# A Hedgehog linear-attention and Mish MLP block: the head rebuilt around ScalarE's roots, loads re-queued and held, three later orders changed

## The chip, the core and the metric

One Trainium2 chip, one core. The metric is the device time of one execution in microseconds (us); lower is better. TensorE is called PE, VectorE DVE, ScalarE ACT, GpSimd POOL; SyncE (SP) only issues DMAs here, and ACT has a DMA queue of its own beside its compute.

## What is computed

For x of 2048 tokens by 512 channels (bf16), with 32 heads of 16:

```python
xn = layernorm(x)                                  # eps 1e-5
q, k, v = split(xn @ wqkv)                         # 32 heads of 16
pq, pk = q @ w_phi[h], k @ w_phi[h]                # per head, 16x16
phi = concat(softmax(p), softmax(-p))              # for q and for k, 32 features
kv, z = sum over tokens of phi_k^T v, phi_k        # no causal mask
o  = (phi_q @ kv) / (phi_q @ z + 1e-6)
h  = xn @ w1 + b1                                  # 512 -> 1792
out = x + o @ wo + mish(h) @ w2                    # mish(h) = h*tanh(softplus(h))
```

## The kernel before

**Tiles and groups.** The tokens are 16 tiles of 128 (`x_sb[:, t, :]`), in NG = 4 groups of TPG = 4. xn is needed transposed (`xnT`); the first group is transposed on PE (`ln_turn_pe`: four 128x128 transposes into a PSUM bank, then a copy), the others by DMA (`ln_turn_dma`).

**Folded weights.** w_phi acts per head, so `fold` multiplies the keys' part of wqkv (loaded transposed by DMA, `load_turned`, tile `wT`) with a block-diagonal w_phi (`Wbd`, the product of a 0/1 mask `block` and the loaded `wsrc`). The result `wkp` gives pk directly from xn: `logits(s, i)` is four accumulating matmuls (`project`) and a cast to `p_sb`. Later `wqp` is made alike for the queries. Steps s = 0 to 3 are the keys' groups, s = 4 to 7 the queries' groups.

**Softmaxes.** `extremes(s)` finds each head's maximum and minimum by a tree on DVE and writes p - max and min - p to `e`; `exponentials` runs Exp on ACT in halves of two tiles (and, for the queries, `turn` transposes each tile by DMA into `qT`); `normalise` sums and divides on DVE for the keys. `accumulate` sums kv in PSUM.

**MLP.** `hidden(n)` does the next n of 56 units: four matmuls with w1 and a Mish on ACT, per 128 hidden channels and group of tokens. They are the filler between the attention's steps: 5, then for s = 0 6+6+5, then 14, 8, 10, and 2 after the last group. `second_layer(t, f0, f1)` adds 128x512 matmuls with w2 for tile t.

**Second phase.** A half h is two tiles. `attend(h, i)` makes numerator and denominator in four PSUM banks (`pnd`, one buffer) and ACT copies them out; `combine` divides on DVE and transposes by DMA (`ob`); `project_out(h)` adds the product with wo, `residual` adds x on DVE, and `store` issues what waits.

**Order.** The order on each engine is the order of the program (a manual schedule): nothing is reordered. PSUM banks come from pools in fixed rotations: a matmul into a bank waits until the copy of its last use is done. In the second phase the second-layer blocks and the projections rotate over four banks (`ps`).

**The head** (lines 438 to 494). SP issues tiles 0 and 1 of x, then the transposed keys' weights, then tiles 4 to 7, wv, w1 and tiles 8 to 15. ACT issues w_phi, tiles 2 and 3, and b1. PE runs 12 warm-up matmuls on the identity (L466) until the data are there. Variance to 1/sqrt runs on POOL (L131: add eps, L134: power of -0.5); DVE makes `Wbd` (L472). Then PE does the fold (L110), transposes of tiles 0 and 1 (L152), the first projection (L168), the transposes of tiles 2 and 3, three more projections, the values (from 13.11 us) and the hidden units.

Of the kernel before, what the change touches and what calls it, by code (L numbers as in the profile page):

```python
# [9 lines left out]
BF16 = mybir.dt.bfloat16  # L10
# [8 lines left out]
def kernel(  # L19
# [13 lines left out]
    P = 128  # L33
# [54 lines left out]
    wo_sb = wqk[:, :, D : 2 * D]  # L88
    ident = consts.tile([P, P], BF16, name="ident")
    mhalf = consts.tile([P, TPG], FP32, name="mhalf")  # L90
    block = consts.tile([P, 8, 16], BF16, name="block")
    KVmask = consts.tile([P, 34], FP32, name="KVmask")
    vext = [vpool.tile([P, TPG, 4, 4, 36], BF16, name=f"vext{i}") for i in range(2)]
# [5 lines left out]
    def load_turned(base_col):  # L99

        wT = lnp.tile([P, 4, 512], BF16, name="wT", tag="xn")
        nc.sync.dma_start_transpose(out=wT[:], in_=A_wqkv[:, base_col : base_col + D])
        return wT

    def fold(wT, dst, dve):

        for kt in range(KT):
            pf = bank("pfold")
            for j in range(4):
                nc.tensor.matmul(  # L110
                    pf[:, j * P : (j + 1) * P],
                    lhsT=wT[:, j, kt * P : (kt + 1) * P],
                    rhs=Wbd[:, j, :],
                    start=True,
                    stop=True,
                )
            if kt in dve:
                nc.vector.tensor_copy(dst[:, kt, :], pf[:])
            else:
                nc.scalar.copy(dst[:, kt, :], pf[:])  # L120

    def ln_stats(t0, n):

        stats = lnp.tile([P, TPG, nc.vector.BN_STATS_DIM], FP32, name="stats")
        mv = lnp.tile([P, TPG, nc.vector.BN_AGGR_DIM], FP32, name="mv")
        rstd = lnp.tile([P, TPG], FP32, name="rstd")
        for i in range(n):
            nc.vector.bn_stats(stats[:, i, :], x_sb[:, t0 + i, :])  # L128
        for i in range(n):
            nc.vector.bn_aggr(mv[:, i, :], stats[:, i, :])  # L130
        nc.gpsimd.tensor_scalar(  # L131
            out=rstd[:, 0:n], in0=mv[:, 0:n, 1], scalar1=1e-5, scalar2=None, op0=ALU.add
        )
        nc.gpsimd.tensor_tensor(out=rstd[:, 0:n], in0=rstd[:, 0:n], in1=mhalf[:, 0:n], op=ALU.pow)  # L134
        return mv, rstd
# [24 lines left out]
            in_=xn[:, i : i + 2, :].rearrange("p t c -> p (t c)"),  # L160
        )

    def project(w, t, pp=None):

        if pp is None:
            pp = bank("pproj")[:]
        for kt in range(KT):
            nc.tensor.matmul(  # L168
                pp, lhsT=xnT[:, t, kt, :], rhs=w[:, kt, :],
                start=(kt == 0), stop=(kt == KT - 1),  # L170
            )
        return pp
# [65 lines left out]
                    op=ALU.subtract,  # L238
                )

    def exponentials(s, ks=(0, 1)):
        for k in ks:
            v = e_of[s][:, 2 * k : 2 * k + 2, :, :]
            nc.scalar.activation(v, v, ACT.Exp)  # L244
            if s >= NG:
                turn(s, k)

    def turn(s, k):

        qT = epool.tile([P, 2, 8, P], BF16, name="qT", bufs=3)  # L250
        qT_of[2 * (s - NG) + k] = qT
        for i in range(2):
            nc.sync.dma_start_transpose(
                out=qT[:, i, :, :],
                in_=e_of[s][:, 2 * k + i, :, :].rearrange("p l c -> p (l c)"),
            )

    def normalise(s, k, between=None):

# [155 lines left out]
    def project_out(h):  # L415
        for t in (2 * h, 2 * h + 1):
            for po, c in zip(po_of.pop(t), halves(t)):
                for j in range(4):
                    nc.tensor.matmul(  # L419
                        po[:, c], lhsT=oT_of[h][:, t % 2 * 4 + j, :], rhs=wo_sb[:, j, c],  # L420
                        start=False, stop=(j == 3),
                    )
                residual(t, po, c, nc.scalar if c.stop == 256 else nc.sync)

    def residual(t, po, c, queue):
        y = x_sb[:, t, c]
        nc.vector.tensor_tensor(out=y, in0=po[:, c], in1=y, op=ALU.add)  # L427
        waiting.append((queue, o_v[:, t, c], y))

    waiting = []  # L430

    def store():
        while waiting:
            queue, to, y = waiting.pop(0)
            queue.dma_start(to, y)


    nc.sync.dma_start(x_sb[:, 0:2, :], x_v[:, 0:2, :])
    with nc.allow_non_contiguous_dma(reason="tiny w_phi load"):
        nc.scalar.dma_start(wsrc[:], wphi_v)  # L440
    wT = load_turned(D)
    nc.scalar.dma_start(x_sb[:, 2:4, :], x_v[:, 2:4, :])
    nc.scalar.dma_start(b1b[:], b1_v[:, :])
    nc.sync.dma_start(x_sb[:, 4:8, :], x_v[:, 4:8, :])
    nc.sync.dma_start(wv[:], wqkv_v[:, :, 2 * D : 3 * D])
    nc.sync.dma_start(w1_sb[:], w1_v[:, :, :])
    nc.sync.dma_start(x_sb[:, 8:16, :], x_v[:, 8:16, :])


    make_identity(nc, ident[:])  # L450

    nc.gpsimd.memset(block[:], 1.0)
    for sign in (1, -1):
# [8 lines left out]
    dve, act = nc.vector.tensor_copy, nc.scalar.copy  # L462

    warm = bank("warm")
    for _ in range(12):
        nc.tensor.matmul(  # L466
            warm[:].rearrange("p (k c) -> p k c", k=4), lhsT=ident[:], rhs=ident[:, None, :].to_broadcast([P, 4, P]),
            start=True, stop=True,
        )

    st0 = ln_stats(0, 2)
    nc.vector.tensor_tensor(  # L472
        out=Wbd[:].rearrange("p j (h e) -> p j h e", h=8),
        in0=block[:, None, :, :].to_broadcast([P, 4, 8, 16]),
        in1=wsrc[:, :, None, :].to_broadcast([P, 4, 8, 16]),
        op=ALU.mult,
    )
    st1 = ln_stats(2, 2)
    xn = lnp.tile([P, TPG, D], BF16, name="xn", tag="xn")
    ln_apply(0, 2, *st0, xn, 0)  # L480
    fold(wT, wkp, (3,))
    ln_turn_pe(0, xn, 0, dve)
    ln_turn_pe(1, xn, 1, act)
    pb = bank("pb", BF16)
    nc.tensor.transpose(pb[:, 0:FT], b1b[:], ident[0:FT, 0:FT])
    ln_apply(2, 2, *st1, xn, 2)
    logits(0, 0, act)
    for i in range(2, 4):
        ln_turn_pe(i, xn, i, dve)
    nc.vector.tensor_copy(b1f[:], pb[:, 0:FT])  # L490
    for i in range(1, TPG):
        logits(0, i, act)

    def normal(t0, st, xn):
        ln_apply(t0, TPG, *st, xn, 0)
# [7 lines left out]
    nc.sync.dma_start(wo_sb, wo_v[:, :, :])  # L503
    for i in range(TPG):
        value(i, act)
    hidden(5)

    for s in range(NG):
        exponentials(s, (0, 1) if s else (0,))
        if s > 0:  # L510
            accumulate(s - 1, pk)
        if s < NG:
            for i in range(2 if s else 0):
                value(s * TPG + i, dve)
        if s == 0:
            p_of[1] = smx.tile([P, TPG, 512], BF16, name="p_sb", bufs=1)
            act(p_of[1][:, 0, :], project(wkp, TPG))
            exponentials(0, (1,))
            stack, pool = three_banks("pw", 1)
            wide = pool.tile([P, 3, 512], FP32, name="pwide", tag="wide")  # L520
            for i in range(3):
                project(wkp, TPG + 1 + i, wide[:, i, :])
        else:
            for i in range(TPG):
                logits(s + 1, i, act)
        if 0 < s < NG:
# [151 lines left out]
```

## Time and profile before

| | us |
|---|---|
| median of 3 runs (lowest, highest) | 180.5 (180.41, 180.91) |
| the profiled execution, its time | 180.89 |
| its span, first to last instruction | 178.8 |

| engine | busy us | share of the span |
|---|---|---|
| DVE | 151.9 | 85% |
| ACT | 123.9 | 69% |
| POOL | 29.6 | 17% |

The profile is of one execution. A timeline line reads: start, duration, engine, line of the kernel, operation, output<-inputs, shapes, count, and in brackets the idle time of the engine before it and what ended it. `ACTq` and `SPq` are DMA issues on that engine's queue. A 128x512 matmul is shown with about 0.38 us, its time through the pipeline; the next one starts about 0.216 us later, so starts say more than durations. The chain of waits follows the last instruction back, at each step to what released it. Between 45 and 97 us PE is busy for 51.84 and DVE for 49.10 of 52.00 us.

### The profile page before, as it was taken

Reading aid. Unit: us, or ns where it says so; the run is one execution under the profiler, and the core shown is the slowest. Engines: PE = TensorE matmul, PEld = TensorE weight load, DVE = VectorE, ACT = ScalarE, POOL = GpSimd, SP = SyncE. Lnnn points to the kernel's source line nnn. Section 1 sums busy time; section 2 is a strip of 40 time slices with the busy share of each in tenths; the row PEclk is TensorE's granted clock in tenths of the full one; section 3 lists DMA queues with packets and bytes.
Section 4 is the critical chain, followed back from the end, with each engine's and each line's share of the span. In section 5 each row is a group of like instructions: output and inputs, shape, how many; then the busy total and the mean of one; then the engine's idle time right before and its main releaser. Section 6 shows DMA issues by size and latency. Waiting matters only on the chain.

```text
span 178.8 us, 4304 instructions
## 1 busy us (share of the span) xinstructions
PE 171.7 (96%) x1785; PEld 82.3 (46%) x1807; DVE 151.9 (85%) x297; ACT 123.9 (69%) x162; POOL 29.6 (17%) x42
## 2 busy tenths in 40 slices
PE   6899999999999999999999999999999999998993
PEld 2554443445444545454454444444444444444561
DVE  1989979996999989998999979699789978797844
ACT  2357999999998799969994989389322863543200
POOL 4404059500699500000000000000000000000000
PEclk9999999999999999999999999999999999999999
DMA  6997796310013600000000492909946069386344
GB/s 149 294 412 267 130 339 198 69 31 4 4 23 75 141 0 0 4 4 0 0 0 4 91 148 59 121 5 153 208 125 106 0 129 138 88 81 159 64 101 134
DMA packets 44527, 18.12 MB, mean 101 GB/s; under 512 B 36956, under 2 KB 43996, under 8 KB 44508
## 3 DMA queue, kind: packets, MB, share of 16 engines
q1 hardware_dynamic: 43536, 17.50, 44.9%
q10 hardware_dynamic: 972, 0.35, 0.7%
q8 instruction: 14, 0.23, 0.6%
q14 instruction: 5, 0.04, 0.1%
HBM read 6.84 MB, written 2.10 MB: 50 GB/s over the span
## 4 chain that ended last, share of the span: by engine, by line
PE 47%; DVE 37%; ACT 8%; DMA 4%; issue 2%; POOL 0%; DVEq 0%; POOLq 0%; ACTq 0%; SPq 0%
PE po L410 21%; DVE s L262 7%; PE po L419 7%; DVE m L225 6%; PE ph L189 6%; PE pproj L168 5%; ACT e L244 5%; DVE e L234 5%; DVE e L275 4%; DVE stats L128 4%; DVE r L270 3%; PE warm L466 3%; PE pnd L337 2%; DMA qT<-e 2%; DMA ob<-ob 2%
## 5 line engine op out<-in xcount | busy, mean ns | idle before, releaser
L410 PE MATMUL po<-w_sb,acts 128*128 128x512 bf16 (+1 forms) x224 | 50.2, 366 | 0.8 <-PE pnd L337 0.2
L189 PE MATMUL ph<-xnT,w_sb 128*128 128x512 bf16 x224 | 49.5, 379 | 0.3 <-ACT acts L196 0.3
L196 ACT ACTIVATE acts<-ph,b1f 128x512 bf16<-128x512 f32 x56 | 34.7, 706 | 2.0 <-PE ph L189 1.9
L244 ACT ACTIVATE e<-e 128x2048 bf16<-128x2048 bf16 x16 | 30.2, 1911 | 6.4 <-DVE e L234 6.3
L189 PEld LDWEIGHTS <-w_sb 128*128 128x128 bf16 x224 | 21.8, 98 | 26.7 <-issue 0.6
L410 PEld LDWEIGHTS <-acts 128*128 128x128 bf16 x238 | 22.1, 98 | 22.5
L168 PEld LDWEIGHTS <-xnT 128*128 128x128 bf16 x192 | 18.1, 98 | 21.9 <-DMA xnT<-xn 0.9
L262 DVE TENSOR_REDUCE s<-e 128x128 f32<-128x2048 bf16 x8 | 18.2, 2277 | 2.5 <-ACT e L244 2.5
L427 DVE TENSOR_TENSOR x_sb<-po,x_sb 128x512 bf16<-128x512 f32 (+1 forms) x17 | 11.0, 659 | 7.5 <-PE po L419 7.4
L347 ACT COPY ds<-pnd 128x128 f32<-128x128 f32 x16 | 4.4, 275 | 18.0 <-PE pnd L337 15.7
L140 POOL TENSOR_SCALAR xn<-x_sb,mv,rstd 128x512 bf16<-128x512 bf16 x8 | 16.7, 2102 | 0.2
L419 PE MATMUL po<-wqk,ob 128*128 128x512 bf16 (+1 forms) x67 | 14.9, 367 | 0.5 <-DMA ob<-ob 0.4
L168 PE MATMUL pproj<-wv,xnT 128*128 128x512 bf16 x61 | 14.8, 379 | 0.2
L225 DVE TENSOR_TENSOR m<-m 128x256 bf16<-128x256 bf16 (+2 forms) x44 | 13.4, 305 | 1.5
L168 PE MATMUL pproj<-wqk,xnT 128*128 128x512 bf16 x62 | 14.4, 379 | 0.1
L209 ACT CAST p_sb<-pproj 128x512 bf16<-128x512 f32 x21 | 11.3, 587 | 4.1 <-PE pproj L168 4.1
L128 DVE BATCH_NORM_STATS2 stats<-x_sb 128x6 f32<-128x512 bf16 x16 | 10.0, 679 | 3.7 <-DMA x_sb<-in_A_x_dram 3.7
L168 PE MATMUL pproj<-wkp,xnT 128*128 128x512 bf16 x50 | 11.8, 379 | 0.1
L275 DVE TENSOR_TENSOR e<-e,r 128x2048 bf16<-128x2048 bf16 x8 | 10.3, 1282 | 0.3
L225 DVE TENSOR_TENSOR m<-p_sb 128x1024 bf16<-128x1024 bf16 (+1 forms) x18 | 10.2, 567 | 0.0
L419 PEld LDWEIGHTS <-ob 128*128 128x128 bf16 x68 | 6.5, 98 | 7.3 <-DMA ob<-ob 0.5
L234 DVE TENSOR_TENSOR e<-p_sb,m 128x2048 bf16<-128x2048 bf16 (+1 forms) x9 | 8.9, 989 | 0.3
(65 smaller groups left out, 172.9 us busy)
## 6 DMA issues: line engine op xcount, KB each, us to landing
w_sb<-in_B_w_dram SPq DMA_DIRECT2D x2, 1792.0 KB, 8.5
out_dram<-x_sb SPq DMA_DIRECT2D x15, 128.0 KB, 1.9
x_sb<-in_A_x_dram SPq DMA_DIRECT2D x1, 1024.0 KB, 10.9
x_sb<-in_A_x_dram SPq DMA_DIRECT2D x1, 512.0 KB, 4.0
wv<-in_A_wqkv_dram SPq DMA_DIRECT2D x1, 512.0 KB, 4.9
wqk<-in_A_wo_dram SPq DMA_DIRECT2D x1, 512.0 KB
x_sb<-in_A_x_dram SPq DMA_DIRECT2D x1, 256.0 KB, 2.9
x_sb<-in_A_x_dram ACTq DMA_DIRECT2D x1, 256.0 KB, 3.5
```

Of the source, the lines that this page charges most:

```text
L128: nc.vector.bn_stats(stats[:, i, :], x_sb[:, t0 + i, :])
L140: engine.tensor_scalar(out=xn[:, at + i, :], in0=x_sb[:, t0 + i, :], scalar1=mv[:, i, 0:1], scalar2=rstd[:, i : i + 1], op0=ALU.subtract, ...
L168: nc.tensor.matmul(pp, lhsT=xnT[:, t, kt, :], rhs=w[:, kt, :], start=(kt == 0), stop=(kt == KT - 1),)
L189: nc.tensor.matmul(ph[:], lhsT=w1_sb[:, kt, f * P : (f + 1) * P], rhs=xnT[:, g * TPG : (g + 1) * TPG, kt, :], start=(kt == 0), stop=(kt == ...
L196: nc.scalar.activation(acts[:, f, g * 512 : (g + 1) * 512], ph[:], ACT.Mish, bias=b1f[:, f : f + 1])
L225: nc.vector.tensor_tensor(out=m, in0=src[:, :, 0:half], in1=src[:, :, half : 2 * half], op=op)
L234: nc.vector.tensor_tensor(out=e[:, :, pl, :].rearrange("p t (c e o) -> p t c e o", e=8, o=2), in0=p5 if pl == 0 else mb, in1=mb if pl == 0 ...
L244: nc.scalar.activation(v, v, ACT.Exp)
L262: nc.vector.reduce_sum(t[:], v.rearrange("p t l (c e) -> p (t l c) e", e=16), axis=AX.X)
L275: nc.vector.tensor_tensor(out=vv, in0=vv, in1=r2[:, :, None, :].to_broadcast([P, 128, 8, 2]), op=ALU.mult)
L410: nc.tensor.matmul(po[:, c], lhsT=acts[:, f, t * P : (t + 1) * P], rhs=w2_sb[:, f, c], start=(f == 0), stop=False,)
L419: nc.tensor.matmul(po[:, c], lhsT=oT_of[h][:, t % 2 * 4 + j, :], rhs=wo_sb[:, j, c], start=False, stop=(j == 3),)
```

## The change

What it does, in the order of the program:

1. **Loads.** SP issues the keys' weights (transposed) first. ACT issues w_phi, tiles 0 and 1, tiles 2 and 3, and b1. A one-column copy on POOL from `wsrc` into tile 4 of `x_sb` stands before the load of tiles 4 to 7, so that SP's later loads wait for w_phi.
2. **Norms of the first group** (`spread` statistics, `gather` aggregates, `deviate` root, `invert` reciprocal, `apply` writes xn). The standard deviation comes from ACT (`Sqrt` with eps as bias, after an early `Sqrt` on a constant), the reciprocal from DVE, tile by tile for tiles 0 and 1 and together for 2 and 3. POOL keeps the later groups.
3. **`Wbd`** is made on POOL.
4. **Order of the head.** 11 warm-ups; the transposes of tile 0 come before the fold; the fold's casts are ACT, ACT, DVE, ACT; the second projection is split around the transposes of tile 2. The head has its own rotation of eight banks.
5. **Middle.** Six hidden units instead of five before s = 0 and four instead of five at its end; the cast of the first projection of group 1 is on DVE.
6. **Step 4** (first queries): the first half's Exp is done tile by tile, each followed by its transpose; `attend(0, 0)` comes right after the two hidden units, two second-layer matmuls earlier.
7. **Tail.** `combine(5)` is done tile by tile, with two transposes; all stores are issued by SP (before, the first half of the last tile's store was on ACT's queue).

The diff, cut to its core:

```diff
-    def exponentials(s, ks=(0, 1)):
+    def exponentials(s, ks=(0, 1), singly=()):
...
-            nc.scalar.activation(v, v, ACT.Exp)
-            if s >= NG:
-                turn(s, k)
+            for n in range(1 + (k in singly)):
+                m = 2 - (k in singly)
+                t = 2 * k + n
+                v = e_of[s][:, t : t + m, :, :]
+                nc.scalar.activation(v, v, ACT.Exp)
+                for i in range(t, t + m):
+                    if s >= NG:
+                        turn(s, k, i)
...
-    nc.sync.dma_start(x_sb[:, 0:2, :], x_v[:, 0:2, :])
+    wT = load_turned(D)
     with nc.allow_non_contiguous_dma(reason="tiny w_phi load"):
         nc.scalar.dma_start(wsrc[:], wphi_v)
-    wT = load_turned(D)
-    nc.scalar.dma_start(x_sb[:, 2:4, :], x_v[:, 2:4, :])
+    for t in (0, 2):
+        nc.scalar.dma_start(x_sb[:, t : t + 2, :], x_v[:, t : t + 2, :])
     nc.scalar.dma_start(b1b[:], b1_v[:, :])
...
     make_identity(nc, ident[:])
+    nc.gpsimd.memset(eps[:], 1e-5)
+    nc.scalar.activation(root[:], eps[:], ACT.Sqrt)
...
+    nc.gpsimd.tensor_copy(x_sb[:, 4, 0:1], wsrc[:, 0, 0:1])
     nc.sync.dma_start(x_sb[:, 4:8, :], x_v[:, 4:8, :])
...
-    nc.vector.tensor_tensor(
+    nc.gpsimd.tensor_tensor(
         out=Wbd[:].rearrange("p j (h e) -> p j h e", h=8),
...
+    head, hd = three_banks("hd", 3)
+    turns[0] = cycle([hd, ps, hd, px, ps, hd, ps, ps])
     warm = bank("warm")
-    for _ in range(12):
+    for _ in range(11):
...
+    def deviate(t, n):
+        nc.scalar.activation(rstd[:, t : t + n], mv[:, t : t + n, 1], ACT.Sqrt, bias=eps[:])
...
+    for t in (0, 1):
+        spread(t)
+        gather(t, 1)
+        deviate(t, 1)
+    for t in (0, 1):
+        invert(t, 1)
+        apply(t)
+    ln_turn_pe(0, xn, 0, act)
+    spread(2)
+    spread(3)
+    gather(2, 2)
+    fold(wT, wkp, (), (0, 1))
+    deviate(2, 2)
+    fold(wT, wkp, (2,), (2, 3))
+    ln_turn_pe(1, xn, 1, dve)
+    invert(2, 2)
+    apply(2)
+    apply(3)
+    logits(0, 0, act)
+    p1 = project(wkp, 1, kts=range(0, 2))
+    ln_turn_pe(2, xn, 2, dve)
+    act(p_of[0][:, 1, :], project(wkp, 1, p1, kts=range(2, 4)))
+    ln_turn_pe(3, xn, 3, dve)
...
-    hidden(5)
+    hidden(6)
...
-            act(p_of[1][:, 0, :], project(wkp, TPG))
+            dve(p_of[1][:, 0, :], project(wkp, TPG))
...
-        hidden((5, 14, 8, 10)[s])
+        hidden((4, 14, 8, 10)[s])
...
-    exponentials(4)
+    exponentials(4, singly=(0,))
...
-    second_layer(1, 0, 2)
     attend(0, 0)
-    second_layer(1, 2, 12)
+    second_layer(1, 0, 12)
...
-    combine(5)
+    combine(5, first)
+    combine(5, last)
```

More of the change, by code (lines that the diff above doesn't have):

```diff
@@ L90 @@
     mhalf = consts.tile([P, TPG], FP32, name="mhalf")
+    eps = consts.tile([P, 1], FP32, name="eps")
+    root = consts.tile([P, 1], FP32, name="root")
     block = consts.tile([P, 8, 16], BF16, name="block")
@@ L103, in load_turned, with fold @@
         return wT
-    def fold(wT, dst, dve):
-        for kt in range(KT):
+    def fold(wT, dst, dve, kts=range(KT)):
+        for kt in kts:
             pf = bank("pfold")
@@ L161, in ln_turn_dma, with project @@
         )
-    def project(w, t, pp=None):
+    def project(w, t, pp=None, kts=range(KT)):
         if pp is None:
             pp = bank("pproj")[:]
-        for kt in range(KT):
+        for kt in kts:
             nc.tensor.matmul(
@@ L239, in extremes, with turn @@
                 )
-    def exponentials(s, ks=(0, 1)):
+    def exponentials(s, ks=(0, 1), singly=()):
         for k in ks:
-            v = e_of[s][:, 2 * k : 2 * k + 2, :, :]
-            nc.scalar.activation(v, v, ACT.Exp)
-            if s >= NG:
-                turn(s, k)
[L248 to L256, printed above, removed]
+            for n in range(1 + (k in singly)):
[6 more added lines that the diff above has]
+                        turn(s, k, i)
+    def turn(s, k, i):
+        h = 2 * (s - NG) + k
+        if i == 2 * k:
+            qT_of[h] = epool.tile([P, 2, 8, P], BF16, name="qT", bufs=3)
+        nc.sync.dma_start_transpose(
+            out=qT_of[h][:, i - 2 * k, :, :],
+            in_=e_of[s][:, i, :, :].rearrange("p l c -> p (l c)"),
+        )
     def normalise(s, k, between=None):
@@ L422, in project_out, with residual @@
                     )
-                residual(t, po, c, nc.scalar if c.stop == 256 else nc.sync)
-    def residual(t, po, c, queue):
+                residual(t, po, c)
+    def residual(t, po, c):
         y = x_sb[:, t, c]
         nc.vector.tensor_tensor(out=y, in0=po[:, c], in1=y, op=ALU.add)
-        waiting.append((queue, o_v[:, t, c], y))
+        waiting.append((o_v[:, t, c], y))
     waiting = []
@@ L433, in store @@
         while waiting:
-            queue, to, y = waiting.pop(0)
-            queue.dma_start(to, y)
-    nc.sync.dma_start(x_sb[:, 0:2, :], x_v[:, 0:2, :])
+            nc.sync.dma_start(*waiting.pop(0))
+    wT = load_turned(D)
     with nc.allow_non_contiguous_dma(reason="tiny w_phi load"):
         nc.scalar.dma_start(wsrc[:], wphi_v)
-    wT = load_turned(D)
-    nc.scalar.dma_start(x_sb[:, 2:4, :], x_v[:, 2:4, :])
+    for t in (0, 2):
+        nc.scalar.dma_start(x_sb[:, t : t + 2, :], x_v[:, t : t + 2, :])
     nc.scalar.dma_start(b1b[:], b1_v[:, :])
[L444 to L447, printed above, removed]
     make_identity(nc, ident[:])
+    nc.gpsimd.memset(eps[:], 1e-5)
+    nc.scalar.activation(root[:], eps[:], ACT.Sqrt)
     nc.gpsimd.memset(block[:], 1.0)
@@ L461 @@
         nc.gpsimd.memset(vext[i][:, :, :, :, 32:36], 1.0)
-    dve, act = nc.vector.tensor_copy, nc.scalar.copy
-    warm = bank("warm")
-    for _ in range(12):
[L466 to L471, printed above, removed]
-    nc.vector.tensor_tensor(
+    nc.gpsimd.tensor_copy(x_sb[:, 4, 0:1], wsrc[:, 0, 0:1])
+    nc.sync.dma_start(x_sb[:, 4:8, :], x_v[:, 4:8, :])
+    nc.sync.dma_start(wv[:], wqkv_v[:, :, 2 * D : 3 * D])
+    nc.sync.dma_start(w1_sb[:], w1_v[:, :, :])
+    nc.sync.dma_start(x_sb[:, 8:16, :], x_v[:, 8:16, :])
+    nc.gpsimd.tensor_tensor(
         out=Wbd[:].rearrange("p j (h e) -> p j h e", h=8),
@@ L477 @@
     )
-    st1 = ln_stats(2, 2)
-    xn = lnp.tile([P, TPG, D], BF16, name="xn", tag="xn")
[L480 to L483, printed above, removed]
+    dve, act = nc.vector.tensor_copy, nc.scalar.copy
+    head, hd = three_banks("hd", 3)
+    turns[0] = cycle([hd, ps, hd, px, ps, hd, ps, ps])
+    warm = bank("warm")
+    for _ in range(11):
+        nc.tensor.matmul(
+            warm[:].rearrange("p (k c) -> p k c", k=4), lhsT=ident[:], rhs=ident[:, None, :].to_broadcast([P, 4, P]),
+            start=True, stop=True,
+        )
@@ new lines, with spread, gather @@
+    xn = lnp.tile([P, TPG, D], BF16, name="xn", tag="xn")
+    stats = lnp.tile([P, TPG, nc.vector.BN_STATS_DIM], FP32, name="stats")
+    mv = lnp.tile([P, TPG, nc.vector.BN_AGGR_DIM], FP32, name="mv")
+    rstd = lnp.tile([P, TPG], FP32, name="rstd")
+    def spread(t):
+        nc.vector.bn_stats(stats[:, t, :], x_sb[:, t, :])
+    def gather(t, n):
+        for i in range(t, t + n):
+            nc.vector.bn_aggr(mv[:, i, :], stats[:, i, :])
+    def deviate(t, n):
+        nc.scalar.activation(rstd[:, t : t + n], mv[:, t : t + n, 1], ACT.Sqrt, bias=eps[:])
@@ new lines, in invert, with apply @@
+    def invert(t, n):
+        nc.vector.reciprocal(rstd[:, t : t + n], rstd[:, t : t + n])
+    def apply(t):
+        nc.vector.tensor_scalar(
+            out=xn[:, t, :], in0=x_sb[:, t, :], scalar1=mv[:, t, 0:1], scalar2=rstd[:, t : t + 1],
+            op0=ALU.subtract, op1=ALU.mult,
+        )
+    for t in (0, 1):
[8 more added lines that the diff above has]
+    spread(3)
@@ L484 @@
+    gather(2, 2)
[11 more added lines that the diff above has]
+    ln_turn_pe(3, xn, 3, dve)
     pb = bank("pb", BF16)
     nc.tensor.transpose(pb[:, 0:FT], b1b[:], ident[0:FT, 0:FT])
-    ln_apply(2, 2, *st1, xn, 2)
-    logits(0, 0, act)
@@ L488 @@
-    for i in range(2, 4):
-        ln_turn_pe(i, xn, i, dve)
     nc.vector.tensor_copy(b1f[:], pb[:, 0:FT])
-    for i in range(1, TPG):
+    for i in range(2, TPG):
         logits(0, i, act)
+    head.close()
+    turns[0] = cycle([px, ps, ps, ps, ps])
     def normal(t0, st, xn):
```

## The prediction, made before the changed kernel was run

> **What bounds it now.** The page's first part says TensorE (PE); its percentage includes filler, so the timeline of the head comes next, and there the starts are what counts.
>
> ```profile
> PE 171.7 (96%) x1785; PEld 82.3 (46%) x1807; DVE 151.9 (85%) x297; ACT 123.9 (69%) x162; POOL 29.6 (17%) x42
> ```
> ```profile
> 0.79 0.46 SPq L438 DMA_DIRECT2D x_sb<-in_A_x_dram  x1
> 1.30 0.56 ACTq L442 DMA_DIRECT2D x_sb<-in_A_x_dram  x1
> 1.31 3.13 SPq L102 DMA_TRANSPOSE wT<-in_A_wqkv_dram  x1
> ...
> 1.42 5.30 PE L466 MATMUL warm<-ident 128*128 128x512 bf16 x12 [1.42 <-POOL ident masks.py:199]
> ...
> 3.72 1.29 DVE L128 BATCH_NORM_STATS2 stats<-x_sb 128x6 f32<-128x512 bf16 x2 [3.72 <-DMA x_sb<-in_A_x_dram]
> ...
> 6.53 1.47 PE L110 MATMUL pfold<-Wbd,wT 128*128 128x128 bf16 x16
> ...
> 9.20 1.04 PE L168 MATMUL pproj<-wkp,xnT 128*128 128x512 bf16 x4
> ...
> 13.11 3.62 PE L168 MATMUL pproj<-wv,xnT 128*128 128x512 bf16 x16
> ```
>
> Until 6.53 PE does only warm-ups; the first projection starts at 9.20, the values at 13.11, and from there PE has work almost without a gap until 175.9. So a gain must be an earlier 13.11 or a removed PE wait. The timeline between 20 and 46 shows the largest wait, and a slack on VectorE (DVE):
>
> ```profile
> 24.55 4.48 PE L189 MATMUL ph<-xnT,w_sb 128*128 128x512 bf16 x20
> 29.32 1.89 PE L189 MATMUL ph<-xnT,w_sb 128*128 128x512 bf16 x8 [0.29 <-ACT acts L196]
> ```
> ```profile
> 25.02 2.29 DVE L262 TENSOR_REDUCE s<-e 128x128 f32<-128x2048 bf16 x1 [1.10 <-ACT e L244]
> ...
> 41.98 0.69 DVE L176 CAST vext<-pproj 128x512 bf16<-128x512 f32 x1 [1.37 <-PE pproj L168]
> 42.84 0.69 DVE L176 CAST vext<-pproj 128x512 bf16<-128x512 f32 x1 [0.17 <-PE pproj L168]
> ```
>
> Twenty matmuls at 0.216 us (4.48/20, less the last one's tail) should end at 28.86; the next starts at 29.32: PE stood 0.46. From 42.84 to 97.6 the chain of waits is DVE, with ScalarE (ACT) exponentials between, and PE is full beside it: both limits are equal there, so gaining time needs both. At 97 to 106 the chain runs through ACT:
>
> ```profile
> 97.59 1.92 ACT e L244
> ...
> 104.36 0.16 ACT ds L347
> 104.52 0.92 ACT wkp L353
> 105.44 0.04 issue
> 105.48 0.38 PE pnd L337 x32
> ```
>
> Last, PE's timeline near the end:
>
> ```profile
> 163.22 0.37 PE L337 MATMUL pnd<-kvm,qT 32*128 32x36 bf16 x32
> 164.00 1.90 PE L419 MATMUL po<-wqk,ob 128*128 128x512 bf16 x8 [0.41 <-DMA ob<-ob]
> 165.84 0.37 PE L337 MATMUL pnd<-kvm,qT 32*128 32x36 bf16 x32
> 166.14 6.25 PE L410 MATMUL po<-w_sb,acts 128*128 128x512 bf16 x41
> ```
>
> PE waits about 0.48 for the transposed outputs of half 5 (0.78 between starts, where 0.30 is usual).
>
> **First tokens.** Tiles 0 and 1 of x (128 tokens each) move from SyncE's queue (SP; issued 0.79, landed 2.91 later, 3.70) to ACT's, second behind w_phi, where tiles 2 and 3 now stand (issued 1.30, 3.46 to landing, 4.77). Bounds of the new landing: 1.30+2.91 = 4.2 and 4.77. I take 4.3: the present 3.46 was spent beside tiles 0 and 1, which are gone; wT, earlier now, takes their place only late, because its packets (256 bytes) start 2.36 after its issue, 3.67 in the trace.
>
> **Norms.** Removed: POOL's roots for tiles 0 and 1 (0.33+0.73) and 2 and 3 (0.28+0.73). New, from the landing L: statistics 0.68 and aggregate 0.16 end at L+0.9; root on ACT 0.2 to 0.3 (nearest row: 128x128 copy, 0.28); the same for tile 1; reciprocals, by the rows 128x128, x64, x32 at 0.95, 0.55, 0.35, about 0.16 for one column; apply 0.40. First xn ready at L+2.35 = 6.65 (now 7.27). The built program has one table load ahead of the root, in place of the copy's at 2.62 (1.28 us), and none between the root and the copies after it, so nothing is added; behind one more DMA issue (0.56) it ends near 4.5, before the first root at L+0.9.
>
> **Fold and projection.** PE's order is now: 11 warm-ups (0.43 apart, ending 6.12 instead of 6.53), the transposes of tile 0, then the fold. Transposes 6.65 to 7.1; fold from 7.1, if wT is there: issued 0.52 earlier, but sharing the engines with all four tiles; now 6.48, so 6.0 to 6.9. It hides behind the transposes. Then ACT works in a row: xnT copy (7.3 to 7.9), two fold casts, the root of tiles 2 and 3 (it waits for DVE's aggregates, L+4.25 = 8.55, and ACT is free only at 8.9), the last fold cast; at 0.48 to 0.59 each the row ends at L+5.25 = 9.55. Now that last cast ends at 8.75, with DVE's copy of xnT at 9.05. So the first projection ends at 9.8 instead of 10.07. What is left, 12 matmuls of 0.216, 8 transposes in 0.45 and the bias transpose with its wait, 0.15, makes 13.05 against 13.11: gain 0.06. The earlier xn is spent in ACT's row.
>
> **Wbd on POOL and the hold.** DVE loses 0.41. POOL takes it after w_phi (3.88) and a one-column copy (about 0.1 to 0.3). Price between a select of a quarter of its size (0.34) and a two-operation pass over as many elements (2.1): ready 4.5 to 6.3, fold at 7.1: hidden. The Trainium skill's GPSIMD Engine Reference (§3.1) counts about 2.6 cycles per element for two inputs; that is an estimate of 1.1 us, within these bounds. Behind the waiting copy stand the product on POOL and, on SP, tiles 4 to 7, wv, w1 and tiles 8 to 15. SP is busy with wT until 0.79+3.13 = 3.92, so the hold until about 4.1 costs nothing: those loads go 0.4 earlier than 4.50. Behind wT's later bytes they may land 0.45 later: values' weights 10.0, needed at 13; w1 14.5, needed at 16.5. Nothing gained or lost.
>
> **One more hidden unit ahead, DVE for a cast.** The fifth unit's end (20.9) met the transposed second group just as it landed; a sixth adds 0.86 of cover, taken from later (6+6+6+4 against 5+6+6+5). DVE starts its next statistics 0.6 later (its copy of tile 3 ends at L+7.5), the landing at 20.9 becomes 21.5; PE ends its sixth unit at 21.7. DVE, which casts the next group's first projection in ACT's place (0.57 saved there), waits for that projection until 22.8, with the statistics of 8 to 11 queued behind: cast 0.69, statistics and aggregates 2.74, reduction at 26.1 instead of 25.02, that is 1.1 late, so it reaches 41.98's place at 41.7. That uses up the 1.37 of idle. ACT's next table load ends near 28.9 instead of 28.57, with PE's five filled banks until 29.5: of the 0.46 about 0.1 remains, and the small wait near 22.6 (0.14) goes. PE gains 0.5, with the head 0.56; DVE, released by the second value cast, follows by 0.49. If that cover fails, DVE is bound and the gain is lost.
>
> **One exponential in two.** By 512 elements at 0.69 and 2048 at 1.91, 1024 cost 1.1; back to back, ACT's row to 105.48 grows by 0.19. The attention placed earlier only moves PE's wait: its second step needs ACT's copy in either order. Price 0.19; bounds -0.1 (the second copy slips forward) to 0.25.
>
> **Half 5 in two, one queue.** The first half's transpose (2.4 to land) can go only when SP ends qT's issue at 160.44, landing 162.9; the second is ready at 157.07+2x2.33 = 161.7, landing 164.2, used from 164.4. The 0.48 goes. But DVE is 1.0 longer; its half 6 ends at 165.4, so the residual of tile 10 ends 166.15 instead of 165.77, and the next second-layer block reuses that bank: it starts at 166.2, where it starts now. Net +0.05; bounds -0.45 (bank free earlier) to +0.2. The two last stores both from SP: 0.33 issue each, +0.06.
>
> **Sum.** -0.49 +0.19 +0.05 +0.06 = -0.19. The profiled execution took 180.89 (span 178.8 and 2.1 around it), so 180.7 there; it lies 0.39 above the median, and from the median 180.5 comes 180.3. The measurement can tell about 0.3%, 0.54 us.
>
> **Rivals.** (a) The head and the tail pay: tiles at 4.2, the exponential free, the residual in time for its bank: -0.49-0.1+0-0.45+0.06, about -1.0: 179.5. For it: four independent small slacks; against: each must hold.
>
> (b) Slower: PE is still slow when the fold comes. The warm-ups are 0.43 apart, later matmuls of the same size 0.216, with PEclk at 1.00 throughout. The table by stretches, for pfold alone (busy us and count of PE, DVE, ACT; PEclk; DMA share; GB/s), shows the step inside the fold:
>
> ```profile
> 7.00:7.44 0.44, 0.44 (x7) 0.00 (x0) 0.26 (x1) 1.00 1.00 354
> 7.44:7.83 0.39, 0.39 (x10) 0.00 (x0) 0.39 (x2) 1.00 1.10 352
> ```
>
> Both counts take in matmuls that began before the stretch; ten in 0.39 against seven in 0.44 is the step, after six unbroken microseconds. In the changed order PE idles from 6.12 to 6.65, inside that stretch. If the idleness delays the step until about the first projection, the fold doubles (16x0.05) and four matmuls run at 0.43 as the casts arrive: the projection ends near 11.0 instead of 9.8, and all behind it is 1.2 later: 181.5. Needed six microseconds anew, from 6.65, it would be 2.0; I take 1.2, since a gap of 0.5 is small against six. It decides from the length of gap that the step tolerates, which no row shows. The Trainium skill's page TensorE: Matmul & The Clock Gate (Part 1) says that the full clock comes after a busy window of about 3.4 us whose phase is free; by that, some executions would be hit, with a step near 10.8, and others not. The trace's step at 7.44 fits it.
>
> (c) Tiles 0 and 1 land at 4.77 or POOL's product needs more than 2.9: +0.45, 180.8. And the hold may do nothing at all, as above; that is part of the forecast.
>
> **Chances.** Forecast 0.53 (36 within the bound, 10 below, 7 above), (a) 0.24, (b) 0.18 (one of it within), (c) 0.05 (three within, two above). Faster by over 0.3%: 0.10+0.24 = 0.34; within 0.36+0.01+0.03 = 0.40; slower 0.07+0.17+0.02 = 0.26. Range 179.3 to 181.5: (a) with the exponential's bound of -0.1 and 0.1 for the scatter of the runs, and (b); alone the forecast's case is 179.8 to 180.8.
>
> **What would show it.** First statistics at 4.3; fold at 7.1 with matmuls already dense; the values' projection at 13.05; no PE wait near 29; DVE's cast at 41.5 without idle; first pnd near 101.9 but the second near 105.2; the block now at 166.14 unmoved. Values before 12.7, or a first projection after 10.5, would prove the head's sum wrong.

## The result and the profile after

| | before | changed kernel |
|---|---|---|
| median of the runs, us (lowest, highest; runs) | 180.57 (180.41, 180.93; 6) | 182.19 (181.87, 183.25; 6) |
| ratio to before, 95% interval | | 1.0089 [1.0071, 1.0108] |
| profiled execution, us (span) | 180.89 (178.8) | 182.23 (180.3) |

The change makes the kernel slower by 0.9%, about 1.6 us, where 180.3 was forecast. The page's first part hardly moves, and says nothing of the cause:

```profile
PE 172.3 (96%) x1806; PEld 82.0 (45%) x1806; DVE 153.8 (85%) x305; ACT 123.9 (69%) x166; POOL 28.7 (16%) x41
```

The timeline of the head (start, duration, engine, line, operation) does:

```profile
0.79 1.39 SPq L104 DMA_TRANSPOSE wT<-in_A_wqkv_dram  x1
...
1.24 1.05 ACTq L447 DMA_DIRECT2D x_sb<-in_A_x_dram  x2
...
3.08 1.15 POOL L470 TENSOR_TENSOR Wbd<-block,wsrc 128x512 bf16<-128x512 bf16 x1
3.15 0.42 SPq L466 DMA_DIRECT2D x_sb<-in_A_x_dram  x1
...
5.69 0.69 DVE L493 BATCH_NORM_STATS2 stats<-x_sb 128x6 f32<-128x512 bf16 x1 [5.69 <-DMA x_sb<-in_A_x_dram]
...
7.94 0.40 PE L154 MATMUL ptr<-ident,xn 128*128 128x128 bf16 x4 [1.86 <-DVE xn L506]
...
8.18 1.06 PE L112 MATMUL pfold<-Wbd,wT 128*128 128x128 bf16 x16
...
14.13 3.62 PE L170 MATMUL pproj<-wv,xnT 128*128 128x512 bf16 x16
```

The first statistics start at 5.69 (3.72 before), PE stands for 1.86 after its warm-ups, and the values start at 14.13 (13.11). The chain of waits (start, length, what) begins with that load, and the whole head hangs on it:

```profile
1.24 4.42 DMA x_sb<-in_A_x_dram
5.66 0.02 issue
5.69 0.70 DVE stats L493
```

Further on, VectorE's timeline shows the idle ahead of the value casts used up (1.37 before):

```profile
23.83 0.69 DVE L565 CAST p_sb<-pproj 128x512 bf16<-128x512 f32 x1 [1.06 <-PE pproj L170]
...
27.09 2.26 DVE L268 TENSOR_REDUCE s<-e 128x128 f32<-128x2048 bf16 x1
29.39 0.95 DVE L276 RECIPROCAL r<-s 128x128 bf16<-128x128 f32 x1
30.37 0.59 DVE L277 COPY r<-r 128x256 bf16<-128x256 bf16 x1
31.00 1.67 DVE L281 TENSOR_TENSOR e<-e,r 128x2048 bf16<-128x2048 bf16 x1
...
43.31 1.28 DVE L178 CAST vext<-pproj 128x512 bf16<-128x512 f32 x2
```

Here the copy takes 0.59 and the product 1.67. The same two operations before the change, and POOL's four products (one per tile, so some 2.07 each) beside them in the changed kernel:

```profile
28.33 0.29 DVE L271 COPY r<-r 128x256 bf16<-128x256 bf16 x1
28.66 1.23 DVE L275 TENSOR_TENSOR e<-e,r 128x2048 bf16<-128x2048 bf16 x1
```
```profile
28.72 8.29 POOL L142 TENSOR_SCALAR xn<-x_sb,mv,rstd 128x512 bf16<-128x512 bf16 x4
```

PE's timeline at the second attention and near the end:

```profile
106.62 0.38 PE L343 MATMUL pnd<-kvm,qT 32*128 32x36 bf16 x32 [0.60 <-ACT wkp L359]
...
164.68 1.90 PE L425 MATMUL po<-wqk,ob 128*128 128x512 bf16 x8
166.52 0.37 PE L343 MATMUL pnd<-kvm,qT 32*128 32x36 bf16 x32
167.26 6.24 PE L416 MATMUL po<-w_sb,acts 128*128 128x512 bf16 x42 [0.37 <-DVE x_sb L433]
```

The wait for `ob` (0.41 before) is gone, and a wait for the residual of tile 10, which holds the next bank, stands in its place. Seven moments of the traces give the account (us from the start of the span):

| | values | reduction | second reduction | first Exp of step 4 | second pnd | last matmul | last store landed |
|---|---|---|---|---|---|---|---|
| before | 13.11 | 25.02 | 46.11 | 97.59 | 105.48 | 175.59 | 177.94 |
| changed | 14.13 | 27.09 | 47.16 | 98.64 | 106.62 | 176.69 | 179.34 |
| difference | 1.02 | 2.07 | 1.05 | 1.05 | 1.14 | 1.10 | 1.40 |

The loss is made in the head, grows and shrinks in the middle, and 0.30 is added behind the last matmul.

### The profile page after: what moved, and what is told of

Read it like the earlier page. It is cut to its first block, busy times and chain, and to the rows that moved or that the text cites. A ratio compares the mean times of both kernels' runs of the same rounds, so it can differ in the third digit from the quotient of the medians.

```text
span 180.3 us, 4338 instructions
## 1 busy us (share of the span) xinstructions
PE 172.3 (96%) x1806; PEld 82.0 (45%) x1806; DVE 153.8 (85%) x305; ACT 123.9 (69%) x166; POOL 28.7 (16%) x41
## 4 chain that ended last, share of the span: by engine, by line
DVE 47%; PE 41%; DMA 4%; ACT 4%; issue 2%; ACTq 0%; DVEq 0%
PE po L416 21%; DVE s L268 10%; PE pproj L170 8%; PE po L425 6%; DVE m L227 6%; DVE e L281 6%; DVE e L236 5%; DVE r L276 4%; PE ph L191 3%; DVE stats L130 3%; DMA x_sb<-in_A_x_dram 2%; ACT e L249 2%; PE pnd L343 2%; DMA qT<-e 2%; DVE r L277 2%
## 5 line engine op out<-in xcount | busy, mean ns | idle before, releaser
L416 PE MATMUL po<-w_sb,acts 128*128 128x512 bf16 (+1 forms) x238 | 51.0, 367 | 0.4 <-DVE x_sb L433 0.4
L249 ACT ACTIVATE e<-e 128x2048 bf16<-128x2048 bf16 (+1 forms) x17 | 30.2, 1808 | 7.9 <-DVE e L236 7.8
L211 ACT CAST p_sb<-pproj 128x512 bf16<-128x512 f32 x20 | 10.8, 587 | 3.8 <-PE pproj L170 2.3
L170 PE MATMUL pproj<-wkp,xnT 128*128 128x512 bf16 x52 | 12.5, 379 | 0.2
L236 DVE TENSOR_TENSOR e<-m,p_sb 128x2048 bf16<-128x2048 bf16 (+1 forms) x9 | 8.9, 988 | 0.3
```

The source lines that it names most:

```text
L170: nc.tensor.matmul(pp, lhsT=xnT[:, t, kt, :], rhs=w[:, kt, :], start=(kt == 0), stop=(kt == KT - 1),)
L236: nc.vector.tensor_tensor(out=e[:, :, pl, :].rearrange("p t (c e o) -> p t c e o", e=8, o=2), in0=p5 if pl == 0 else mb, in1=mb if pl == 0 ...
L416: nc.tensor.matmul(po[:, c], lhsT=acts[:, f, t * P : (t + 1) * P], rhs=w2_sb[:, f, c], start=(f == 0), stop=False,)
```

## The experiments

Each run is set against executions of the kernel before that were made beside it; their medians were 180.55, 180.59 and 180.61. `values` and the other moments are those of the table above.

**e1: the old loads.** Edit to the changed kernel:

```diff
-    wT = load_turned(D)
+    nc.sync.dma_start(x_sb[:, 0:2, :], x_v[:, 0:2, :])
...
         nc.scalar.dma_start(wsrc[:], wphi_v)
-    for t in (0, 2):
-        nc.scalar.dma_start(x_sb[:, t : t + 2, :], x_v[:, t : t + 2, :])
+    wT = load_turned(D)
+    nc.scalar.dma_start(x_sb[:, 2:4, :], x_v[:, 2:4, :])
```

> The changed kernel with the load order of before: SP issues tiles 0 and 1 of x, then wT; ACT issues w_phi, then tiles 2 and 3. Theory A (the landing of tiles 0 and 1, 5.66 after the change against 3.70 before, is the cost): first statistics near 3.7, fold at about 6.5 when wT lands, values near 12.5 instead of 14.13, time 180.6 to 181.0. Rival B (the new row on ACT, root, copy and casts one after the other, is the cost): values still after 13.6, time 181.8 or more. Rival C (PE slow after the gap behind the warm-ups): no change beyond 0.3 from 182.2.

Measured: 180.87, 1.0023 [1.0014, 1.0032]. Chain of waits and PE's timeline:

```profile
0.79 3.06 DMA x_sb<-in_A_x_dram
```
```profile
6.56 1.07 PE L112 MATMUL pfold<-Wbd,wT 128*128 128x128 bf16 x16
```

The tiles land at 3.85 and the values start at 12.32, 1.81 earlier than in the changed kernel and 0.79 earlier than before the change; the last matmul is 1.89 earlier. By the medians the order of the loads costs 1.32 of the 1.62; in the traces, up to the last matmul, it costs more than the whole loss, and the rest of the new head is a gain. What is left over, slower than before by 0.3 though the head is 0.8 ahead, is looked for below. Nearly half of this 1.1 is the choice of executions: the profiled one of the kernel before took 0.32 more than its median, that of e1 0.18 less.

**e2: the new loads alone.** The reverse edit, in the kernel before.

> The kernel before with only the new load order: SP issues wT first; ACT issues w_phi, tiles 0 and 1, tiles 2 and 3. Theory A: first statistics near 5.7, values 1.5 to 2 later than 13.11, time 181.7 to 182.4. Rival B: the loads alone do little, time 180.6 to 181.0.

Measured: 182.53, 1.0124 [1.0098, 1.015]. Statistics start at 5.67, as in the changed kernel. The loads alone cost 2.0 in the old head, more than the whole change (four of the six runs lie between 182.2 and 182.6, two near 183.7). In its profiled execution the first projection came behind several PE waits and ran slowly:

```profile
9.27 0.40 PE L152 MATMUL ptr<-ident,xn 128*128 128x128 bf16 x4 [0.66 <-DVE xn L140]
10.19 0.58 PE L152 MATMUL ptr<-ident,xn 128*128 128x128 bf16 x4 [0.52 <-DVE wkp L118]
...
10.82 1.89 PE L168 MATMUL pproj<-wkp,xnT 128*128 128x512 bf16 x4
```

This execution is one of the two near 183.7, and the table by stretches (PE's busy us and count, PEclk, DMA share, GB/s) shows PE at half the clock there:

```profile
10.00:11.50 1.50, 1.31 (x7) 0.50 1.06 421
11.50:13.00 1.50, 1.50 (x8) 0.50 1.03 406
```

**e3: tiles 0 and 1 first on ScalarE's queue, w_phi second.** The transposed load stays first on SyncE's.

```diff
+    nc.scalar.dma_start(x_sb[:, 0:2, :], x_v[:, 0:2, :])
     nc.scalar.dma_start(wsrc[:], wphi_v)
-    for t in (0, 2):
-        nc.scalar.dma_start(x_sb[:, t : t + 2, :], x_v[:, t : t + 2, :])
+    nc.scalar.dma_start(x_sb[:, 2:4, :], x_v[:, 2:4, :])
```

> The changed kernel with tiles 0 and 1 ahead of w_phi on ACT's queue, wT still first on SP. Theory A1 (their packets share the DMA engines with the transposing load, whose packets flow first): first statistics still after 5.2, time 181.8 to 182.5. Theory A2 (they stand behind the many small packets of w_phi): first statistics near 4.2, time 180.7 to 181.2.

Measured: 181.12, 1.003 [1.0019, 1.0041].

```profile
3.74 0.70 DVE L493 BATCH_NORM_STATS2 stats<-x_sb 128x6 f32<-128x512 bf16 x1 [3.74 <-DMA x_sb<-in_A_x_dram]
...
7.16 1.05 PE L112 MATMUL pfold<-Wbd,wT 128*128 128x128 bf16 x16 [0.76 <-POOL Wbd L470]
```

Now the tiles land at 3.72 and w_phi, a load of 16 KB, at 5.76 instead of 2.89; the fold waits 0.76 for `Wbd`. So it is not ScalarE's queue, nor the transposing load's being first on the other: whichever load is second on ScalarE's queue lands near 5.7 beside it. The records of the packets fit. In the changed kernel the transposing load's packets (256 bytes) start from 2.19 to 6.12, those of tiles 0 and 1 (1 KB) only from 3.52 to 5.20, and the sixteen of these that start before 4.0 take 251 ns on average, where a 1 KB packet alone takes 46. Before, tiles 2 and 3, as large and also second on ScalarE's queue, had theirs from 3.10 to 4.19. So of the 0.89 between the landings at 4.77 and 5.66, 0.42 is a later beginning, and the rest is that the packets are spread over 1.68 instead of 1.09. In e3 the tiles' packets begin at 1.90, ahead of the transposing load's at 2.70. The Trainium skill's page DMA: Bandwidth & Descriptors (Queues, rings and completion order) says that an engine takes turns between its queues, a packet (there a group of descriptors) at a time. From 4.2 to 4.9 the two kinds start about equally often (183 and 189), as turns would have it; from 3.5 to 4.0 it is 16 against 147, which turns alone do not explain. Why a queue's second load begins so late was not tried.

**e4: 15 warm-ups instead of 11**, to shorten PE's gap before the fold.

> The changed kernel with 15 warm-up matmuls, so that PE works until about 7.8, just before xn is there. Theory A and B: no change, 182.0 to 182.4, since the profile of the changed kernel shows the fold dense already after 1.85 us of idleness. Rival C (in some executions the gap leaves PE slow): the median falls by 0.4 to 1.0 and the scatter shrinks.

Measured: 182.15, 1.0086 [1.0073, 1.0099]; the runs lie between 182.08 and 182.22. The median does not move, so the gap as such is not what costs the 1.6. The scatter does shrink, as rival C had it: none of these four runs is like the changed kernel's one at 183.25 (more on it under rival (b) below).

**f1: old loads, and two queues for the last tile's stores.** To e1 is added:

```diff
-                residual(t, po, c)
+                residual(t, po, c, nc.scalar if c.stop == 256 else nc.sync)
```

> The changed kernel with the old order of loads and the last tile's first half store back on ScalarE's queue. Theory: beside the late tiles, one queue for the stores is the only dear part; it costs 0.25 (in the changed kernel's trace the last store's issue ends 1.34 later than before, the last matmul only 1.10), so 180.87 less 0.25 = 180.6. Rival: the stores cost the 0.06 that was predicted, 180.8, and what eats the head's gain lies between the values and the tail.

Measured: 181.78, 1.0069 [1.0057, 1.0081]: slower by 0.9 where 0.25 less was expected. Two things went against it in its profile. The second half of `ob` came late,

```profile
165.00 1.04 PE L425 MATMUL po<-wqk,ob 128*128 128x512 bf16 x4 [0.94 <-DMA ob<-ob]
```

and the last store landed 3.52 after the last matmul. The two queues alone do not bring them: f2, f4 and h2 below keep the queues, and their last stores land 2.36 after the last matmul. Only one execution was traced, but all five runs are slow (181.53 to 182.26); why is open. The price of one queue is read elsewhere, from the time between the last matmul and the last landing: with one queue 2.65 (changed kernel, e3) and 2.66 (e1, e4), with two 2.36 (before, e2, f2, f4). One queue costs 0.30.

**f2: f1 with the first Exp of step 4 whole again**, and the attention two matmuls later. (The "kernel before this one" in its expectation is f1.)

```diff
-    exponentials(4, singly=(0,))
+    exponentials(4)
...
+    second_layer(1, 0, 2)
     attend(0, 0)
-    second_layer(1, 0, 12)
+    second_layer(1, 2, 12)
```

> The kernel before this one, and the first half's Exp of the first queries whole again with the attention two second-layer matmuls later, as before the change. Theory (the prediction's price 0.19): the second attention step comes 0.2 earlier, PE's wait before it shrinks from 0.7 to about 0.5, 0.1 to 0.2 less than the kernel before this one. Rival: PE was waiting for the transposed second half all along, so the time does not move.

Measured: 180.35, 0.9985 [0.9976, 0.9993], so faster than before the change. Most of its distance from f1 is f1's two delays. The edit itself is read from the first Exp to the second attention step: 7.88 here and 7.89 before the change, 7.97 or 7.98 with the Exp in two (e1, f1, changed kernel). It costs 0.09 there. With POOL's products later (below), the distance is 7.98 with the Exp in two (h1, k3) and 8.00 and 7.99 with it whole (h2, hb), so there it costs nothing.

**f4: f1 with five hidden units ahead, five later, and the cast on ScalarE**, as before the change.

```diff
-    hidden(6)
+    hidden(5)
...
-            dve(p_of[1][:, 0, :], project(wkp, TPG))
+            act(p_of[1][:, 0, :], project(wkp, TPG))
...
-        hidden((4, 14, 8, 10)[s])
+        hidden((5, 14, 8, 10)[s])
```

> Old loads and old store queue, and the middle as before the change: five hidden units ahead and five later, the cast of the second group's first projection on ScalarE. The prediction's step: the sixth unit covers a PE wait near 29 and is worth 0.5, so this is 0.3 to 0.5 slower than the kernel with six units. Rival: VectorE, which takes over a cast of 0.69 and loses another 0.73 to a slow copy and product (0.58 and 1.67 instead of 0.29 and 1.23), is the bound from 43 on, so the sixth unit brings nothing: the same time within 0.2, VectorE idle some 1.4 ahead of the value casts near 41, and the copy and product near 28 at 0.29 and 1.23.

Measured: 180.80, 1.0006 [0.9998, 1.0015]. f1's two delays spoil the comparison by time; the moments can be compared. The head is as early as in f2 (12.41 and 12.38), but the first Exp of step 4 starts at 97.55 (f2 96.87) and the last matmul at 175.57 (174.81). PE's timeline tells where it went:

```profile
20.54 1.04 PE L170 MATMUL pproj<-wkp,xnT 128*128 128x512 bf16 x4 [0.20 <-DMA xnT<-xn]
21.41 1.03 PE L170 MATMUL pwide<-wkp,xnT 128*128 128x512 bf16 x4
23.24 1.90 PE L170 MATMUL pwide<-wkp,xnT 128*128 128x512 bf16 x8 [0.80 <-DMA xnT<-xn]
```

With five units an earlier head only waits longer for the second group's transposed tokens. The sixth unit, with the cast that goes with it, is worth 0.7, and the expectation's rival falls.

**h1: f1 with POOL's products 0.6 later.**

```diff
-        nc.gpsimd.tensor_scalar(
-            out=rstd[:, 0:n], in0=mv[:, 0:n, 1], scalar1=1e-5, scalar2=None, op0=ALU.add
-        )
+        for _ in range(3 if t0 > TPG else 1):
+            nc.gpsimd.tensor_scalar(
+                out=rstd[:, 0:n], in0=mv[:, 0:n, 1], scalar1=1e-5, scalar2=None, op0=ALU.add
+            )
```

> Old loads and old store queue, and two repeats of the small POOL addition (0.23 each) in the norms of groups 2 and 3, so that POOL's four products start about 0.6 later. Theory: VectorE's copy and product are slow (0.58 and 1.67) only where POOL passes from one product to the next within some 0.4 after the copy's start; 0.6 later the copy takes 0.29 and the product 1.23 in both groups, VectorE's chain is 0.73 ahead near 31 and 1.46 near 52, and the time falls by 0 to 1.0, as far as PE, which is as full as VectorE there, can follow. Rival: it is POOL's first product, whatever its phase, or something else in that stretch, that slows them: 0.58 and 1.67 stay and the time does not move.

Measured: 180.85, 1.0009 [0.9998, 1.0021], with runs near 180.3 (three) and near 180.9 (nine). Copy and product take 0.29 and 1.23 in both groups: the theory of the phase stands. The first Exp of step 4 is 0.72 earlier than in f1, PE's two waits before the attention steps are gone, and the last matmul starts at 174.32 (f1: 175.72, e1: 174.80). As in f1 the last store lands late, 3.41 after it, which would explain the two clusters; that is argued, not shown.

**h2: f2 with the same edit on POOL.**

> The fastest kernel so far (old loads, stores from two queues, Exp whole; 180.35) with POOL's four products of groups 2 and 3 started 0.6 later by two repeats of the small POOL addition. Theory: copy 0.29 and product 1.23 in both groups, PE's waits of 0.5 and 0.3 before the two first attention steps shrink by 0.5 to 0.6 in all, 179.8. Rival: the kernel with later POOL products, whose last store landed 3.41 after the last matmul instead of 2.36, shows that something else takes the gain back, 180.3.

Measured: 179.53 (179.49 to 179.66), 0.9941 [0.9929, 0.9952]: the fastest of all, 1.1 below the kernel before. VectorE's timeline, and POOL's beside it:

```profile
27.64 0.95 DVE L277 RECIPROCAL r<-s 128x128 bf16<-128x128 f32 x1
28.62 0.29 DVE L278 COPY r<-r 128x256 bf16<-128x256 bf16 x1
28.95 1.23 DVE L282 TENSOR_TENSOR e<-e,r 128x2048 bf16<-128x2048 bf16 x1
```
```profile
25.52 0.83 POOL L134 TENSOR_SCALAR rstd<-mv 128x4 f32<-128x4 f32 x3 [9.79 <-DVE mv L132]
26.44 1.03 POOL L137 TENSOR_TENSOR rstd<-rstd,mhalf 128x4 f32<-128x4 f32 x1
27.57 9.84 POOL L143 TENSOR_SCALAR xn<-x_sb,mv,rstd 128x512 bf16<-128x512 bf16 x4
```

POOL's four products take 9.84 here, against 8.29 in the changed kernel: the second takes 2.46 and the fourth 3.25. So part of the waiting seems to have moved from VectorE to POOL, and the kernel is faster all the same. The second attention step starts at 104.12 (f2: 104.75), the last matmul at 174.17 (174.81).

**k3: the changed kernel with nothing but that edit.**

> The changed kernel with nothing else than POOL's products of groups 2 and 3 started 0.6 later. Theory: the slow copy and product, 0.73 in each of the two groups, are part of what the changed kernel loses, since VectorE is its bound from 24 to 97: 0.5 to 0.8 less than its 182.2, with PE's wait of 0.76 before the second attention step gone. Rival: only the loads matter, 182.2.

Measured: 181.84 (181.16 to 182.76), 1.0069 [1.0043, 1.0094]. The trace moves as expected: 0.29 and 1.23, no wait before the second attention step, last matmul 0.59 earlier at 176.10. The time does so only in part: three runs lie between 181.2 and 181.5, three between 182.1 and 182.8, and the interval overlaps the changed kernel's. The slower three were granted a mean clock of 0.989 to 0.991, the faster three 1.000. Against the changed kernel's five runs at 0.999 or more (median 182.14) the faster three are 0.9 lower, as the theory had it; but this division was made after the runs were seen, and it rests on three of them.

**hb: the kernel before with the same edit for group 3 alone** (the condition is `t0 > 2 * TPG`).

> The kernel before the change with POOL's products of group 3 alone started 0.6 later (its group 2 shows 0.29 and 1.23 already). Theory: copy and product near 50 at 0.29 and 1.23, VectorE 0.73 ahead, the second attention step up to 0.6 earlier: 180.0 to 180.4. Rival: PE, as full as VectorE from 45 to 97, cannot follow: 180.55.

Measured: 180.14, 0.9978 [0.9967, 0.9988], as the theory had it. The slow copy cost the kernel before something too, in one group: 0.5 by the medians, 0.3 in the traces from the second reduction to the last matmul (129.48 before, 129.19 here). The trace shows one thing more. The head is unedited, yet the values start at 12.83 instead of 13.11: all the fold's matmuls start about 0.056 apart here, where in the profiled execution of the kernel before the first nine start about 0.107 apart. So 0.28 of the 0.79 that e1's head was ahead seems to be that execution's late step.

**e8: the changed kernel without the hold** (the one-column copy on POOL).

> The changed kernel without the one-column copy on POOL, so that SyncE issues tiles 4 to 7 and the later loads as soon as the transposing load is issued, near 2.2 instead of 3.15. The prediction's step: the hold costs and brings nothing, 182.2 within 0.2. Rival: the tiles and weights that come earlier share the engines with tiles 0 and 1 and wT, whose packets ran until 5.66 and 6.79: these land later, and it is 0.3 or more slower.

Measured: 182.49, 1.01 [1.0085, 1.0115]; its interval overlaps the changed kernel's. SyncE issues tiles 4 to 7 at 2.26 instead of 3.15, and nothing else lands differently: tiles 0 and 1 at 5.63 (5.66), 2 and 3 at 7.45 (7.41), wT at 6.67 (6.65), tiles 4 to 7 at 9.07 (8.94). The hold protects nothing. This execution shows something else, in PE's timeline:

```profile
7.91 0.61 PE L154 MATMUL ptr<-ident,xn 128*128 128x128 bf16 x4 [1.61 <-DVE xn L505]
8.31 1.91 PE L112 MATMUL pfold<-Wbd,wT 128*128 128x128 bf16 x16
...
14.69 2.54 PE L170 MATMUL pproj<-wv,xnT 128*128 128x512 bf16 x11
```

The fold's sixteen matmuls start 0.107 apart (0.056 in the changed kernel's profile), and the values come at 14.69, 0.56 later than there with the same landing of the tiles. That is the prediction's rival (b), in one execution; PE's spacing becomes dense only in the first projection, after 10.45.

## Why the prediction was wrong, point by point

**The step that failed: the landing of tiles 0 and 1.** "I take 4.3", between 4.2 and 4.77; it was 5.66, which is 1.36 later than the head's sum was built on. The reason given was that wT "takes their place only late, because its packets (256 bytes) start 2.36 after its issue". Issued first, its packets started 1.40 after the issue (2.19), ahead of the tiles' (3.52) and among them to their end (5.20). A delay that the trace of before showed for a load issued second was carried over to one issued first, and the upper bound, 4.77, was the landing of a load that had no such neighbour. Rival (c) had the right direction with the wrong end.

**What followed from the landing was nearly right.** With L for the landing, the values were put at L+8.75; they came at L+8.47 in the changed kernel and at L+8.47 in e1 (3.85 and 12.32). `Wbd` took 1.15 on POOL, within the bounds, and was hidden. The estimate from the Trainium skill's GPSIMD Engine Reference (§3.1) was 1.1, so the trace agrees. The hold brought nothing.

**The sixth unit.** Its cover was priced at 0.5 and is worth 0.7 (f4 against f2). VectorE's reduction was to be 1.1 late; against the values it was 1.05 late. But then "it reaches 41.98's place at 41.7", which with the values where they came would be 42.78, and it was 43.31: 0.53 more. Without the wait ahead of the reduction, VectorE's copy meets the change-over between two of POOL's products, and the pair costs 0.74 more; this was in no term. So the sentence "if that cover fails, DVE is bound and the gain is lost" came true for another reason: in e1 VectorE has no idle time from 22.0 to 62.8.

**One exponential in two.** 0.19 predicted, 0.09 measured in these kernels.

**Half 5 in two.** The wait for `ob` went, and the residual's bank took its place, as written. From the second pnd to the last matmul 70.11 became 70.07: -0.04 against +0.05.

**One queue for the stores.** 0.06 predicted, 0.30 measured. The last store is issued 1.05 after the last matmul instead of 0.81, behind another on the same queue, and lands 1.60 after its issue instead of 1.54. The sum named an issue of 0.33 each and showed no working for the 0.06.

**Rival (b)** asked whether PE would be slow after the gap. In the changed kernel's profile it was not, after 1.86 of idleness; in e8's it was, after 1.61, and in e2's profile the projection ran at about 0.42 per matmul. In e8 PE had not yet been fast before the gap: its warm-ups were 0.43 apart to the end, and the projection's matmuls became dense near 10.8, where the prediction had put the step for the executions that are hit. In e2 it was fast in the fold (0.055 apart) and fell back to PEclk 0.50 from about 10 to 13. The Trainium skill's page TensorE: Matmul & The Clock Gate (Part 1), by which the phase of the window is free, agrees with both outcomes. The length of the gap alone does not decide, as the rival had supposed. The runs' mean granted clock tells how often: 0.991 in e2's profiled run, the same in the changed kernel's one at 183.25, 0.989 to 0.991 in three of k3's six, and not under 0.997 in any of e4's four or e1's eleven. That these other runs lost the time in the same place is argued, since they have no trace. The median of the changed kernel is not made by it: without the run at 183.25 it is 182.14.

With the measured terms the sum closes: 1.05 at the second reduction, 0.09 for the Exp, -0.04 for half 5 and 0.30 for the queue are 1.40, the difference of the last landings. The medians differ by 1.62; the profiled execution of the kernel before took 0.32 more than its median, about what the late step in its fold cost.

## What to carry to other kernels

A load's landing time belongs to its place among its neighbours, not to the load: when a transposing load is moved ahead, bound the landing of whatever is queued beside it by the slowest landing that the trace shows with those packets around it. A single profiled execution can be off by as much as the effect looked for, here by 0.3, so compare its time with the median first. An idle gap that a change removes may have kept two engines out of step, so look at what runs beside each operation that moves. Price a tail from the last matmul to the last landing, in one number.

## What the runs showed of the hardware that was not expected

**VectorE beside POOL.** The copy (128x256, bf16) and the product behind it (128x2048) take 0.29 and 1.23 while POOL is inside one of its products of 2.07, and 0.58 and 1.67 where POOL passes to the next product about 0.43 after the copy's start. Where the change-over lay 0.78 or more before the copy or 0.77 or more after its start, both were quick. In f4, with POOL's change-over some 0.3 ahead, only the copy was slow (0.59). Two small POOL operations of 0.23 each, which do nothing new, were worth 0.8 (f2 to h2). What the two engines wait for there was not tried. The Trainium skill's page SBUF — State Buffer (Who interferes with whom) speaks of a lock on ports that the two engines share: whichever starts first holds it for the whole instruction, and the other is blocked. It counts a VectorE instruction with two inputs in SBUF, like this product, among those that meet it beside a GpSimd instruction that reads SBUF. In the slow case the copy ends 0.14 after POOL's product, as by that rule. But the product of h2 starts at 28.95, inside a POOL product that runs from 27.57 to 29.65, and takes 1.23, just as at 66.59, where POOL runs none; there the measurement decides.

**The transposing load.** First on SyncE's queue it is issued in 1.38 to 1.41, behind another load in 3.13 to 3.37. In the changed kernel it lands no earlier for being first, at 6.65 against 6.48 before; with tiles 0 and 1 ahead of its packets, in e3, it lands at 5.99.
